# Causal attention and a gated feed-forward on one core: the scores of the two shorter query blocks share banks and one operation, and the work is put in a new order

## The chip, the cores and the metric

One NeuronCore of a Trainium2 chip runs the whole program as one launch. The metric is the device time of that launch in microseconds (us). A core has five engines that run side by side, each through its own list of instructions in order: TensorE (PE; its weight loads are listed apart as PEld), VectorE (DVE), ScalarE (ACT), GpSimd (POOL) and SyncE (SP), which here issues every DMA. A matrix product is written into PSUM, which has eight banks of 512 float32 per partition.

## The reference

Inputs are `q`, `k`, `v` of shape (4, 12, 448, 64) in float32 and four weight matrices in float64. For each batch and head:

```
scores = q @ k.T / 8, the part above the diagonal set to -1e9
attn   = exp(scores - rowmax) / (sum + 1e-9)
x      = attn @ v                       # heads side by side: (1792, 768)
out    = (((x @ w1) * (x @ w2)) @ w3) @ w_out
```

`w1` and `w2` are 768x1024, `w3` is 1024x1024, `w_out` 1024x768; the result is (1792, 768) in float32.

## The kernel before

**What is computed where.** The product `w3 @ w_out` is formed once in float32 (line 780, `w34_mm`), from weights that are loaded as 64-bit words and decoded by ACT, DVE and POOL (lines 681 to 691). Its first phase holds three row blocks at a time in six banks: two of the pool `mm`, three of the four of the pool `sc`, and the bank `av` (lines 804 and 805). It walks over the eight blocks of `w_out` (called wo 0 to wo 7 here) and needs the blocks of `w3` (w3 0 to w3 2) turned by TensorE first (line 768). Later row blocks use the `mm` banks alone.

Attention runs over 24 pairs of heads (function `pair`). A pair loads its Q and K (`turned_whole` for the first two batches, which turns them on TensorE at line 492; `halved` for the last two, which splits them into float16 halves), forms the scores (`scores`), takes the softmax on DVE (line 592), ACT (line 596) and again DVE, ACT and POOL (`inverse`, `soft`), and multiplies with V (`values`, lines 648 and 653, into the bank `av`).

The feed-forward of a batch is `gate` (lines 904 to 906, into banks of `mm` and `tr`) and `project` (lines 964 to 966). These matmuls use the whole 128x128 array and lie between the operations of the pairs.

**The scores of a pair.** Queries come in three blocks of 128 rows, with 128, 256 and 384 keys (c = 0, 1, 2), for each of two heads, and one last block of 64 rows with 448 keys for both heads. Heads share TensorE as two halves of its rows (mode `row`), the last block as quarters (mode `quad`); the product with V uses halves of the columns (mode `col`). Line 635 makes four TensorE operations: blocks c = 2 of both heads, blocks c = 1, the last block, blocks c = 0. Each operation leases its own banks of `sc` (line 568), one for each head, or one for the last block.

**What sets the order.** Nothing is emitted where it is written. Each step is put into a `Program` with a due time, its costs on the engines that can do it, and what it reads and writes. `Program.order` then simulates the five engines and the DMA queue and picks for each engine, whenever it is free, the available step with the smallest due time, less 24 us (`stick`) for a step of the mode that TensorE is in. A change of mode is charged with 0.095 us (`SWITCH`). All due times come from the dictionary `PLAN`. DMAs are steps of SP, charged with bytes over a rate. The order so found is then fixed for each engine; on the chip an engine waits at each instruction until what it needs is there.

**Holding loads back.** `hold(at, g)` (line 448) makes the loads that were added from step `at` on wait, in the planner's simulation, for the load of wo g. `hv` and `h0` of `PLAN` say which: the two halves of V of the first batch wait for wo hv and wo hv + 1, the loads of pair p for wo h0 + p; where there is no such block nothing waits.

Of the kernel before, what the change touches and what calls it, by code (L numbers as in the profile page):

```python
# [23 lines left out]
NEG = -(2.0**120)  # L24

PE, ACT, DVE, POOL, SP = "PE", "ACT", "DVE", "POOL", "SP"
PLAN = dict(nc=10, wstep=3.6064, soft=-6.8718, w0=50.8305, w34=0.7706, ab=1.9504, out=0.6632, gap=-1.6322, lat=44.2335, begin=-91.0074, wlead=70.5419, urgent=-469.9817, flex=370.3401, sc=-41.0893, vo=-494.4237, av=-194.2706, x=-353.7633, qlead=-514.025, rlead=417.269, v0=250.3178, v1=137.6978, gram=2, nf=3, h0=0, hv=1, ns=7, wo0=372.2276, wo1=301.1492, wom=91.9573, w3a=767.9653, w3l=46.2422, wd=-104.1576, wh=-132.8946, wl=1.1959, fin=-10.7242, ev=483.517, po=[7.835, -22.3194, -46.2642, -45.7187, -46.1544, -168.5123, 44.732, 118.2718, -2.1469, -154.505, -36.8352, 4.8443, 45.9944, -62.3407, -59.3789, -141.4965, -13.9926, -146.366, -84.3586, -180.0751, 32.2385, 37.7583, 62.9194, 45.468], wo=[94.042, -8.263, -88.9315, -217.7217, 115.6771, 99.8526, 211.7957, -24.8481], w3=[-158.8005, -50.8167, -61.9442, -32.663, -51.9857, -143.9432, 16.037, 208.3012], tw=[-214.4914, 58.2404, 21.4694, -22.4979, -112.6908, -172.2348, -114.743, -134.9378, -53.1451, -19.9257, -4.9187, -20.2346, -61.9799, -199.5703, -107.2525, -134.2498], slack=0.1918, pflex=136.6935, fq=2, hlead=80.6809, stick=24.2514, wfrom=6)
# [23 lines left out]
class Program:  # L51
# [1 line left out]


    def __init__(self):
        self.ops, self.writer, self.readers, self.modes = [], {}, {}, {}
        self.port, self.lock = set(), set()
        self.banks, self.leased, self.first = {}, [], {}

# [1 line left out]
        l = Lease(pools)  # L61
        return l, l

    def add(self, due, how, reads=(), writes=(), stage=None, mode=None, port=False, lock=False):

        how = how if isinstance(how, list) else [how]
        i = len(self.ops)
        deps = set()
        for k in reads:
            if k in self.writer:  # L70
                deps.add(self.writer[k])
        for k in writes:
            if k in self.writer:
                deps.add(self.writer[k])
            deps.update(self.readers.get(k, ()))
        for k in reads:
            self.readers.setdefault(k, []).append(i)
        for k in writes:
            self.writer[k] = i
            self.readers[k] = []  # L80
        deps.discard(i)
        self.ops.append((round(due + 3.7e-5, 3), how, deps, stage))
        if mode:
            self.modes[i] = mode
        if port:
# [12 lines left out]
    def order(self):  # L98
# [41 lines left out]
        while len(result) < n:  # L140
# [41 lines left out]
            if e == SP:  # L182
                move, turn = cost
                dma_free = max(dma_free, t + (1.275 if turn else 1.1)) + move
                free[e] = max(t + 0.65, dma_free - 0.93) if turn else t + 0.475
                end = dma_free + 0.91
            else:
                end = t + cost
                if e == DVE and i in self.port:
                    if lock_end > t + HELD:  # L190
                        end = lock_end - HELD + cost
                    elif lock_end <= t:
                        end += 0.1 * max(0.0, min(free[POOL], end) - t)
                    port_end = end
                if e == POOL and i in self.lock:
                    end = lock_end = max(t, port_end) + cost
                if e == PE and cost:
                    mode = self.modes.get(i)
                    if mode != last_mode:
                        cost += SWITCH  # L200
                        last_mode = mode
# [36 lines left out]
def t_mm(n, least=0):  # L238
    return max(n / 2.4 + 2, least) / 1000
# [3 lines left out]
def tile_causal_attention_moe(ctx: ExitStack, tc: tile.TileContext, q, k, v, w1, w2, w3, wo, out):  # L243
# [214 lines left out]
    def take_v(b, half, due):  # L458
# [22 lines left out]
    def turned_whole(p, b, hs, T, qk, qkk, qt, qtk):  # L481

        for i, src in ((1, k), (0, q)):
            dma(qk[0:QP, i], src[b, hs].rearrange("h (p r) d -> p r h d", r=4),
                T - PLAN["qlead"], (), [qkk + (i,)], 2 * S * D * 4, rate=181e3)

        for i in (1, 0):
            ps, key = prog.lease("sc", "tr")
# [12 lines left out]
    def halved(p, b, hs, T, qk, qkk, qt, qtk):  # L501
# [4 lines left out]
        for i, src in ((1, k), (0, q)):  # L506
            raw_k = [qkk + (i, n) for n in range(3)]
            for h in range(2):
                dma(qk[:, i, 0:3, h], src[b, hs.start + h, 0 : 3 * P].rearrange("(c p) d -> p c d", p=P), T - PLAN["qlead"],
                    [], [raw_k[h]], 3 * P * D * 4, rate=181e3)  # L510
            dma(qk[0:D, i, 3], src[b, hs, 3 * P : S].rearrange("h p d -> p h d"), T - PLAN["qlead"],
                [], [raw_k[2]], 2 * D * D * 4, rate=181e3)
# [23 lines left out]
    def pair(p):  # L536
# [25 lines left out]

            return (u // 3, u % 3, (u % 3 + 1) * P, OFF[u % 3]) if u < 6 else (2, 3, S, 0)

        def scores(us, due):
            i, c, w, lo = place(us[0])
            n = min(P, S - c * P)
            banks = [prog.lease("sc") for _ in us]
            m = mask_t if i == 2 else mask[:, (2 - c) * P :]

            def products(qs, ks, start, stop):
                for j in range(2):
                    rows = slice(j * D, (j + 1) * D)
                    ps = banks[j if i < 2 else 0][0]
                    nc.tensor.matmul(ps[rows if i == 2 else slice(0, P), :w], qs[rows, c * P : c * P + n], ks[rows, 0:w],  # L575
                                     start=start, stop=stop)

            def both():
                if not halves:
                    products(qt[:, 0], qt[:, 1], True, True)  # L580
                    return
                q16 = qt.rearrange("p i f -> p (i f)").bitcast(F16).rearrange("p (i t f) -> p i t f", i=2, t=2)
                for m_, (a, b_) in enumerate(((0, 0), (0, 1), (1, 0))):
                    products(q16[:, 0, a], q16[:, 1, b_], m_ == 0, m_ == 2)

            outs = [heads[place(u)[0]] for u in us]
            prog.add(due, (PE, (3 if halves else 4) * t_mm(w) + 0.02, both), [qtk + (1,), qtk + (0,)],
                     [key for _, key in banks] + [tk + (c,) for _, tk in outs] + ([tk for _, tk in outs] if p < 2 else []),
                     mode="quad" if i == 2 else "row")
            for u, (ps, key), (t32, tk) in zip(us, banks, outs):  # L590
                o = t32[:, lo : lo + w]
                prog.add(due + 0.4, (DVE, t_dve(w) + 0.07, lambda o=o, ps=ps, u=u: nc.vector.tensor_tensor_reduce(  # L592
                    out=o, in0=ps[:, :w], in1=m, scale=iv, scalar=-NEG,
                    op0=ALU.add, op1=ALU.min, accum_out=mx[:, u : u + 1])),
                    [key, ivk, "mask_t" if i == 2 else "mask"], [mk + (u,), tk + (c,)] + ([tk] if p < 2 else []))
                prog.add(due + 0.9, (ACT, t_act(w, pointers=1, acc=True), lambda o=o, u=u: nc.scalar.activation(  # L596
                    out=o, in_=o, func=AF.Exp, scale=-1.0, bias=mx[:, u : u + 1], accum_out=sm[:, u : u + 1])),
                    [mk + (u,)], [tk + (c,), smk + (u,)])

        def inverse(us, due):  # L600
            n = slice(us[0], us[-1] + 1)
# [463 lines left out]
```

## Time and profile before

| what | us |
|---|---|
| median of 3 runs (lowest, highest) | 557.48 (556.45, 559.26) |
| the profiled execution, its own time | 555.84 |
| its span, first to last instruction | 554.0 |
| TensorE busy | 537.5 (97%) |
| VectorE busy | 384.4 (69%) |
| ScalarE busy | 323.9 (58%) |
| GpSimd busy | 156.1 (28%) |

A line of the page names the line of the kernel, the engine, the operation, what it writes and reads, how often it ran, and its busy time and mean duration. Matmuls overlap in the records: one is listed from its start until its result has left the array, so a row of 128x448 lasts 0.35 us although the next one starts 0.19 us later. What an operation costs TensorE is read from start to start.

### The profile page before, as it was taken

Reading aid. Unit: us, or ns where it says so; the run is one execution under the profiler, and the core shown is the slowest. Engines: PE = TensorE matmul, PEld = TensorE weight load, DVE = VectorE, ACT = ScalarE, POOL = GpSimd, SP = SyncE. Lnnn points to the kernel's source line nnn. Section 1 sums busy time; section 2 is a strip of 40 time slices with the busy share of each in tenths; the row PEclk is TensorE's granted clock in tenths of the full one; section 3 lists DMA queues with packets and bytes.
Section 4 is the critical chain, followed back from the end, with each engine's and each line's share of the span. In section 5 each row is a group of like instructions: output and inputs, shape, how many; then the busy total and the mean of one; then the engine's idle time right before and its main releaser. Section 6 shows DMA issues by size and latency. Waiting matters only on the chain.

```text
span 554.0 us, 10756 instructions
## 1 busy us (share of the span) xinstructions
PE 537.5 (97%) x3872; PEld 300.5 (54%) x3872; DVE 384.4 (69%) x1057; ACT 323.9 (58%) x774; POOL 156.1 (28%) x118
## 2 busy tenths in 40 slices
PE   2999999999999999999999999999999999999996
PEld 1565565555554555555445555655555555555564
DVE  5536999998999899984998768398986760322100
ACT  6757888798698978654664646265762551111111
POOL 4000465554566424430334203231421110000000
PEclk9999999999999999999999999999999999999999
DMA  8998599989989648998777958979899235000011
GB/s 324 289 298 233 118 217 206 229 215 240 184 216 239 153 97 151 180 178 167 107 155 142 166 128 167 185 164 159 142 142 143 61 84 115 0 2 1 14 58 43
DMA packets 224950, 84.60 MB, mean 153 GB/s; under 512 B 205952, under 2 KB 221824, under 8 KB 224896
## 3 DMA queue, kind: packets, MB, share of 16 engines
q1 hardware_dynamic: 224896, 83.91, 72.1%
q8 instruction: 30, 0.49, 0.4%
q14 instruction: 24, 0.20, 0.1%
HBM read 43.78 MB, written 5.51 MB: 89 GB/s over the span
## 4 chain that ended last, share of the span: by engine, by line
PE 82%; DVE 9%; ACT 3%; DMA 3%; issue 1%; POOL 1%; POOLq 0%; ACTq 0%
PE sc L575 8%; PE mm L780 8%; PE mm L904 7%; PE mm L905 7%; PE mm L906 7%; PE mm L964 5%; PE mm L966 4%; PE mm L965 4%; PE tr L904 4%; PE av L653 4%; PE tr L905 4%; PE tr L906 4%; PE sc L780 2%; PE tr L964 2%; PE tr L966 2%; PE tr L965 2%
## 5 line engine op out<-in xcount | busy, mean ns | idle before, releaser
L906 PE MATMUL mm<-xt,w 128*128 128x448 f16 x258 | 90.9, 352 | 1.3 <-DVE w L727 1.3
L904 PE MATMUL mm<-xt,w 128*128 128x448 f16 x258 | 91.1, 353 | 0.0
L905 PE MATMUL mm<-xt,w 128*128 128x448 f16 x258 | 90.9, 352 | 0.0
L596 ACT ACTIVATE p<-p,mx 128x384 f32<-128x384 f32 (+2 forms) x144 | 71.5, 497 | 28.7 <-DVE mx L592 28.6
L780 PE MATMUL mm<-wof,w3t 128*128 128x384 f32 x192 | 71.4, 505 | 2.5 <-POOL wof L688 2.5
L628 DVE SCALAR_TENSOR_TENSOR ph<-p,rc,ph 128x384 f16<-128x384 f32 (+2 forms) x144 | 68.6, 528 | 1.4 <-ACT ph L623 0.9
L625 POOL TENSOR_SCALAR ph<-p,rc 128x128 f16<-128x128 f32 (+2 forms) x40 | 43.1, 1086 | 69.8 <-DVE rc L606 39.5
L575 PE MATMUL sc<-qkt 64*128 64x384 f16 (+7 forms) x480 | 58.9, 356 | 0.2 <-DMA qkt<-da 0.2
L906 PEld LDWEIGHTS <-w 128*128 128x128 f16 x384 | 37.5, 98 | 37.1 <-DVE w L727 2.2
L904 PEld LDWEIGHTS <-w 128*128 128x128 f16 x384 | 37.5, 98 | 36.0 <-issue 3.5
L905 PEld LDWEIGHTS <-w 128*128 128x128 f16 x384 | 37.5, 98 | 29.7 <-issue 0.2
L964 PE MATMUL mm<-w34h,arena 128*128 128x384 f16 x152 | 49.7, 327 | 0.0
L966 PE MATMUL mm<-w34h,arena 128*128 128x384 f16 x152 | 49.5, 326 | 0.0
L965 PE MATMUL mm<-w34l,arena 128*128 128x384 f16 x152 | 49.5, 326 | 0.0
L780 PEld LDWEIGHTS mm<-wof,w3t 128*128 128x128 f32 x192 | 34.2, 193 | 24.3 <-issue 4.1
L904 PE MATMUL tr<-xt,w 128*128 128x448 f16 x126 | 44.5, 353 | 0.0
L905 PE MATMUL tr<-xt,w 128*128 128x448 f16 x126 | 44.4, 352 | 0.0
L906 PE MATMUL tr<-xt,w 128*128 128x448 f16 x126 | 44.4, 352 | 0.0
L592 DVE CUSTOM_DVE_ANT_0 p<-sc,mask,qiv 128x384 f32<-128x384 f32 (+2 forms) x72 | 31.4, 478 | 18.0 <-PE sc L575 17.8
L930 ACT CAST arena<-g 128x448 f16<-128x448 f32 x22 | 12.4, 563 | 49.2 <-DVE g L925 49.2
L623 ACT ACTIVATE ph<-p,rc 128x384 f16<-128x384 f32 (+2 forms) x64 | 29.1, 504 | 9.5 <-issue 5.7
L685 DVE TENSOR_SCALAR da<-da 128x768 int32<-128x768 int32 (+1 forms) x38 | 24.2, 639 | 14.9 <-ACT da L681 14.7
(182 smaller groups left out, 1028.8 us busy)
## 6 DMA issues: line engine op xcount, KB each, us to landing
arena<-in_moe_w_dram SPq DMA_DIRECT2D x11, 768.0 KB, 5.7
vr<-in_v_dram SPq DMA_DIRECT2D x24, 192.0 KB, 3.9
out_dram<-osb SPq DMA_DIRECT2D x24, 192.0 KB, 2.2
arena<-in_moe_w_dram SPq DMA_DIRECT2D x8, 512.0 KB, 5.1
xt<-in_moe_w_dram SPq DMA_DIRECT2D x5, 768.0 KB, 8.0
qkr<-in_k_dram SPq DMA_DIRECT2D x12, 224.0 KB, 6.3
qkr<-in_q_dram SPq DMA_DIRECT2D x12, 224.0 KB, 6.9
arena<-in_moe_w_out_dram SPq DMA_DIRECT2D x3, 768.0 KB, 9.3
```

The source lines that it names most:

```text
L575: nc.tensor.matmul(ps[rows if i == 2 else slice(0, P), :w], qs[rows, c * P : c * P + n], ks[rows, 0:w], start=start, stop=stop)
L592: prog.add(due + 0.4, (DVE, t_dve(w) + 0.07, lambda o=o, ps=ps, u=u: nc.vector.tensor_tensor_reduce(out=o, in0=ps[:, :w], in1=m, scale=iv, ...
L596: prog.add(due + 0.9, (ACT, t_act(w, pointers=1, acc=True), lambda o=o, u=u: nc.scalar.activation(out=o, in_=o, func=AF.Exp, scale=-1.0, b ...
L625: (POOL, 1.1 * (t_pool(w) + 0.35e-3 * w + 0.16), lambda src=src, r=r, h=h: nc.gpsimd.tensor_scalar(out=h, in0=src, scalar1=r, scalar2=None ...
L628: prog.add(due + 0.4, (DVE, t_dve(w) + 0.06, lambda src=src, r=r, h=h, l=l: nc.vector.scalar_tensor_tensor(out=l, in0=src, scalar=r, in1=h ...
L780: prog.add(due, (PE, 4 * t_mm(NH), lambda: nc.tensor.matmul(ps[:, :NH], w3t[slot(m)][:, g], wof[:, g, ns], start=g == 0, stop=g == KF - 1) ...
L904: nc.tensor.matmul(ps[:, :S], w[:, 0, d], xh, start=d == 0, stop=False)
L905: nc.tensor.matmul(ps[:, :S], w[:, 0, d], xl, start=False, stop=False)
L906: nc.tensor.matmul(ps[:, :S], w[:, 1, d], xh, start=False, stop=d == KD - 1)
L964: nc.tensor.matmul(t, gh[:, fc, cs], w34h[:, fc, ns], start=fc == 0, stop=False)
L965: nc.tensor.matmul(t, gh[:, fc, cs], w34l[:, fc, ns], start=False, stop=False)
L966: nc.tensor.matmul(t, gl[:, fc, cs], w34h[:, fc, ns], start=False, stop=fc == KF - 1)
```

## The change

Three things change.

1. `scores` takes groups of blocks. Line 635 becomes three operations: c = 2; then c = 1 and c = 0 as one operation; then the last block. Block c = 0 (128 columns) is written behind block c = 1 (256 columns) in the same bank, for each head. The last block may lease a bank of `tr` as well as of `sc`. Reads by DVE and ACT stay as they were, one for each block and head.
2. `h0` goes from 0 to -1 and `hv` from 1 to 0: the loads of pair 0 wait for no block of `w_out`, those of pair p for wo p - 1, the halves of V for wo 0 and wo 1.
3. All numbers of `PLAN` are new, and the planner charges DMAs with other rates: 430e3 in place of 330e3 bytes per us, and 230e3 in place of 181e3 for Q, K and V. `SWITCH` stays. Those that bear on what follows:

| `PLAN` | before | after |
|---|---|---|
| h0, hv | 0, 1 | -1, 0 |
| w0, w34, lat, begin | 50.83, 0.7706, 44.23, -91.01 | 99.96, 0.5381, 87.96, 68.00 |
| qlead, rlead, v0 | -514.0, 417.3, 250.3 | -953.2, 432.6, 792.5 |
| wo0, wo1 | 372.2, 301.1 | 423.3, 333.6 |
| first three of w3 | -158.8, -50.8, -61.9 | -367.4, 320.5, 65.3 |
| first four of wo | 94.0, -8.3, -88.9, -217.7 | -105.3, 105.5, -110.6, 1.9 |
| first three of po | 7.8, -22.3, -46.3 | 51.9, -54.4, -3.5 |
| sc, stick | -41.09, 24.25 | -41.22, 25.15 |

```diff
-    def dma(dst, src, due, reads, writes, size, turn=False, rate=330e3):
+    def dma(dst, src, due, reads, writes, size, turn=False, rate=430e3):
...
-                NP * rows * D * 4, rate=181e3)
+                NP * rows * D * 4, rate=230e3)
...
-        def scores(us, due):
-            i, c, w, lo = place(us[0])
-            n = min(P, S - c * P)
-            banks = [prog.lease("sc") for _ in us]
-            m = mask_t if i == 2 else mask[:, (2 - c) * P :]
...
+        def scores(groups, due):
+
+            blocks = []
+            for us in groups:
+                i, c, w, lo = place(us[0])
+                if c == 0:
+                    shared, at = blocks[-1][1], blocks[-1][2] + blocks[-1][4][2]
+                else:
+                    shared, at = [prog.lease("sc") if i < 2 else prog.lease("sc", "tr") for _ in us], 0
+                blocks.append((us, shared, at, mask_t if i == 2 else mask[:, (2 - c) * P :], (i, c, w, lo)))
...
-                    nc.tensor.matmul(ps[rows if i == 2 else slice(0, P), :w], qs[rows, c * P : c * P + n], ks[rows, 0:w],
+                    nc.tensor.matmul(ps[rows if i == 2 else slice(0, P), at : at + w], qs[rows, c * P : c * P + n], ks[rows, 0:w],
...
+            prog.add(due, (PE, cost, both), [qtk + (1,), qtk + (0,)],
+                     list(keys.values()) + [tk + (c,) for tk, c in outs] + ([tk for tk, _ in outs] if p < 2 else []),
+                     mode=mode[0], leave=mode[-1])
...
-                    out=o, in0=ps[:, :w], in1=m, scale=iv, scalar=-NEG,
+                        out=o, in0=ps[:, at : at + w], in1=m, scale=iv, scalar=-NEG,
...
-        for n, us in enumerate(((2, 5), (1, 4), (6,), (0, 3))):
-            scores(us, T + PLAN["sc"] + 0.6 * n)
+        for n, groups in enumerate(([[(2, 5)], [(1, 4), (0, 3)], [(6,)]], [[(2, 5), (6,)], [(1, 4), (0, 3)]])[PLAN["join"]]):
+            scores(groups, T + PLAN["sc"] + 0.6 * n)
```

## Rows read from the trace of the kernel before

**Rows 1.** The page, part 1: busy us (share of the span) and instructions.

```profile
PE 537.5 (97%) x3872; PEld 300.5 (54%) x3872; DVE 384.4 (69%) x1057; ACT 323.9 (58%) x774; POOL 156.1 (28%) x118
```

**Rows 2.** Stretches: span part, then each engine's busy time, clock, DMA share, GB/s.

```profile
0.00:20.00 20.00, 9.51 (x30) 5.82 (x31) 12.08 (x22) 14.60 (x22) 5.58 (x14) 1.00 0.94 329
...
140.00:160.00 20.00, 18.96 (x157) 10.50 (x156) 19.97 (x49) 15.78 (x33) 11.58 (x6) 1.00 0.93 189
...
540.00:560.00 20.00, 9.78 (x61) 5.68 (x58) 0.00 (x0) 1.74 (x3) 0.00 (x0) 0.98 0.12 32
```

**Rows 3.** Waits of TensorE: total us, times, longest.

```profile
PE tr L768 <- DVE arena L688: 6.7, 1, 6.7
PE mm L780 <- POOL wof L688: 2.5, 1, 2.5
PE mm L906 <- DVE w L727: 1.3, 2, 1.0
```

**Rows 4.** Timeline of TensorE, one pair's scores: start, us, line, operation, count.

```profile
284.64 0.35 PE L905 MATMUL tr<-xt,w 128*128 128x448 f16 x1
284.83 0.35 PE L906 MATMUL tr<-xt,w 128*128 128x448 f16 x1
285.12 0.99 PE L575 MATMUL sc<-qkt 64*128 64x384 f16 x12
286.04 0.36 PE L904 MATMUL tr<-xt,w 128*128 128x448 f16 x1
...
288.07 0.34 PE L575 MATMUL sc<-qkt 64*128 64x128 f16 x6
288.34 0.20 PE L407 MATMUL sc<-vam,ones 128*128 128x1 bf16 x2
```

**Rows 5.** Timeline of TensorE: first lone c = 0, one behind the last block.

```profile
55.46 0.49 PE L575 MATMUL sc<-qkt 64*128 64x128 f32 x4
...
432.08 0.35 PE L906 MATMUL tr<-xt,w 128*128 128x448 f16 x1
432.36 1.03 PE L575 MATMUL sc<-qkt 64*64 64x448 f16 x12
433.32 0.36 PE L904 MATMUL tr<-xt,w 128*128 128x448 f16 x1
```

**Rows 6.** VectorE by line and form: one block's read of scores.

```profile
L592 DVE CUSTOM_DVE_ANT_0 p<-sc,mask,minus 128x256 f32<-128x256 f32 x24 | 10.7, 474 | 0.0
```

**Rows 7.** Timeline of SP: the DMAs that it issues, by array.

```profile
12.21 3.21 SPq L443 DMA_DIRECT2D xt<-in_moe_w_out_dram  x1
15.47 5.91 SPq L443 DMA_DIRECT2D vr<-in_v_dram  x4
```

**Rows 8.** Timeline of TensorE, the start.

```profile
12.01 2.93 PE L780 MATMUL mm<-wof,w3t 128*128 128x384 f32 x4 [2.46 <-POOL wof L688]
...
16.47 0.66 PE L768 MATMUL tr<-ident,arena 128*128 128x128 f32 x4 [0.68 <-ACT w3t L774]
...
18.26 1.45 PE L780 MATMUL mm<-wof,w3t 128*128 128x384 f32 x4
...
21.66 0.55 PE L492 MATMUL sc<-ident,qkr 112*128 112x112 f32 x4
22.05 0.82 PE L780 MATMUL mm<-wof,w3t 128*128 128x384 f32 x2
...
23.45 0.97 PE L575 MATMUL sc<-qkt 64*64 64x448 f32 x4
24.34 0.91 PE L780 MATMUL av<-wof,w3t 128*128 128x384 f32 x2
```

**Rows 9.** Five-microsecond stretches, columns as in rows 2.

```profile
10.00:15.00 5.00, 2.99 (x6) 1.66 (x7) 4.57 (x6) 4.47 (x7) 3.13 (x2) 1.00 1.03 424
...
20.00:25.00 5.00, 5.00 (x26) 2.86 (x25) 1.39 (x2) 3.25 (x6) 0.00 (x0) 1.00 1.31 225
```

**Rows 10.** Timeline of VectorE: the last step of decoding wo 2.

```profile
20.25 0.96 DVE L688 CUSTOM_DVE_ANT_0 wof<-arena,da 128x1536 uint16<-128x1536 uint16 x1 [0.25 <-ACT arena L683]
```

More of the change, by code (lines that the diff above doesn't have):

```diff
@@ L26 @@
 PE, ACT, DVE, POOL, SP = "PE", "ACT", "DVE", "POOL", "SP"
[L27 removed]
+PLAN = dict(nc=10, wstep=4.3513, soft=-125.7919, w0=99.9575, w34=0.5381, ab=2.3129, out=0.5532, gap=78.1363, lat=87.9611, begin=67.9975, wlead=196.6466, urgent=-299.9763, flex=910.9122, sc=-41.2246, vo=-404.2803, av=-49.0005, x=-259.5767, qlead=-953.2158, rlead=432.6325, v0=792.4525, v1=218.16, gram=2, nf=3, h0=-1, hv=0, ns=7, wo0=423.2529, wo1=333.6298, wom=-315.019, w3a=862.914, w3l=54.4892, wd=-93.5688, wh=450.671, wl=-765.9963, fin=-205.9569, ev=501.987, po=[51.9383, -54.4417, -3.4751, -73.8006, -93.2459, -608.6472, 37.5565, 81.3517, 120.7744, -301.2995, 17.1976, -6.3764, -50.4787, -37.7123, 53.8748, -159.4007, -388.994, -287.5193, -157.9855, -515.3219, 71.1529, 55.4979, -137.0095, 90.513], wo=[-105.2729, 105.5246, -110.6113, 1.9064, 375.9098, -133.5289, 485.9559, 384.1313], w3=[-367.4466, 320.5192, 65.304, -211.3003, 54.027, -253.7773, -188.4862, 3.6743], tw=[-29.043, 60.8811, -87.4584, 146.6723, 18.5679, -292.661, -259.0009, -29.9851, -211.3435, -155.3741, -12.1051, 43.4863, 65.5179, -660.2283, -57.2076, -236.7873], slack=0.8159, pflex=192.9167, fq=2, hlead=120.4329, stick=25.1509, wfrom=6, join=0)
 HOP = {
@@ L55, in __init__ @@
     def __init__(self):
-        self.ops, self.writer, self.readers, self.modes = [], {}, {}, {}
+        self.ops, self.writer, self.readers, self.modes, self.leave = [], {}, {}, {}, {}
         self.port, self.lock = set(), set()
@@ L62, in lease, with add @@
         return l, l
-    def add(self, due, how, reads=(), writes=(), stage=None, mode=None, port=False, lock=False):
+    def add(self, due, how, reads=(), writes=(), stage=None, mode=None, leave=None, port=False, lock=False):
         how = how if isinstance(how, list) else [how]
@@ L84, in add @@
             self.modes[i] = mode
+            self.leave[i] = leave or mode
         if port:
@@ L200, in order @@
                         cost += SWITCH
-                        last_mode = mode
+                    last_mode = self.leave.get(i)
                     end = matmul(t, cost)
@@ L484, in turned_whole @@
             dma(qk[0:QP, i], src[b, hs].rearrange("h (p r) d -> p r h d", r=4),
-                T - PLAN["qlead"], (), [qkk + (i,)], 2 * S * D * 4, rate=181e3)
+                T - PLAN["qlead"], (), [qkk + (i,)], 2 * S * D * 4, rate=230e3)
         for i in (1, 0):
@@ L509, in halved @@
                 dma(qk[:, i, 0:3, h], src[b, hs.start + h, 0 : 3 * P].rearrange("(c p) d -> p c d", p=P), T - PLAN["qlead"],
-                    [], [raw_k[h]], 3 * P * D * 4, rate=181e3)
+                    [], [raw_k[h]], 3 * P * D * 4, rate=230e3)
             dma(qk[0:D, i, 3], src[b, hs, 3 * P : S].rearrange("h p d -> p h d"), T - PLAN["qlead"],
-                [], [raw_k[2]], 2 * D * D * 4, rate=181e3)
+                [], [raw_k[2]], 2 * D * D * 4, rate=230e3)
             flat = qk[:, i].rearrange("p c h d -> p (c h d)")
@@ L563, in place, with products @@
             return (u // 3, u % 3, (u % 3 + 1) * P, OFF[u % 3]) if u < 6 else (2, 3, S, 0)
-        def scores(us, due):
-            i, c, w, lo = place(us[0])
-            n = min(P, S - c * P)
-            banks = [prog.lease("sc") for _ in us]
-            m = mask_t if i == 2 else mask[:, (2 - c) * P :]
-            def products(qs, ks, start, stop):
+        def scores(groups, due):
[7 more added lines that the diff above has]
+                blocks.append((us, shared, at, mask_t if i == 2 else mask[:, (2 - c) * P :], (i, c, w, lo)))
+            def products(block, qs, ks, start, stop):
+                us, banks, at, _, (i, c, w, lo) = block
+                n = min(P, S - c * P)
                 for j in range(2):
@@ L582, in both @@
[L582 to L589, printed above, removed]
@@ L590, in scores @@
-            for u, (ps, key), (t32, tk) in zip(us, banks, outs):
-                o = t32[:, lo : lo + w]
-                prog.add(due + 0.4, (DVE, t_dve(w) + 0.07, lambda o=o, ps=ps, u=u: nc.vector.tensor_tensor_reduce(
-                    out=o, in0=ps[:, :w], in1=m, scale=iv, scalar=-NEG,
[L594 to L598, printed above, removed]
+                for block in blocks:
+                    if not halves:
+                        products(block, qt[:, 0], qt[:, 1], True, True)
+                        continue
+                    q16 = qt.rearrange("p i f -> p (i f)").bitcast(F16).rearrange("p (i t f) -> p i t f", i=2, t=2)
+                    for m_, (a, b_) in enumerate(((0, 0), (0, 1), (1, 0))):
+                        products(block, q16[:, 0, a], q16[:, 1, b_], m_ == 0, m_ == 2)
@@ new lines, in scores @@
+            keys = {id(l): l for b_ in blocks for _, l in b_[1]}
+            outs = [(heads[place(u)[0]][1], b_[4][1]) for b_ in blocks for u in b_[0]]
+            mode = ["quad" if b_[4][0] == 2 else "row" for b_ in blocks]
+            cost = sum((3 if halves else 4) * t_mm(b_[4][2]) + 0.02 for b_ in blocks) + SWITCH * (mode[0] != mode[-1])
+            prog.add(due, (PE, cost, both), [qtk + (1,), qtk + (0,)],
+                     list(keys.values()) + [tk + (c,) for tk, c in outs] + ([tk for tk, _ in outs] if p < 2 else []),
+                     mode=mode[0], leave=mode[-1])
@@ new lines, in scores @@
+            for us, banks, at, m, (i, c, w, lo) in blocks:
+                for u, (ps, key) in zip(us, banks):
+                    t32, tk = heads[place(u)[0]]
+                    o = t32[:, lo : lo + w]
+                    prog.add(due + 0.4, (DVE, t_dve(w) + 0.07, lambda o=o, ps=ps, u=u, at=at, w=w, m=m: nc.vector.tensor_tensor_reduce(
+                        out=o, in0=ps[:, at : at + w], in1=m, scale=iv, scalar=-NEG,
+                        op0=ALU.add, op1=ALU.min, accum_out=mx[:, u : u + 1])),
+                        [key, ivk, "mask_t" if i == 2 else "mask"], [mk + (u,), tk + (c,)] + ([tk] if p < 2 else []))
+                    prog.add(due + 0.9, (ACT, t_act(w, pointers=1, acc=True), lambda o=o, u=u: nc.scalar.activation(
+                        out=o, in_=o, func=AF.Exp, scale=-1.0, bias=mx[:, u : u + 1], accum_out=sm[:, u : u + 1])),
+                        [mk + (u,)], [tk + (c,), smk + (u,)])
```

3 lines of the change are left out of this document (removed).

## The prediction

> **What bounds the kernel now.** The page's busy times come first: TensorE is busy 537.5 of 554.0 us, VectorE, next, 384.4 [rows 1]. The stretches show where TensorE is not: 10.5 us are missing in the first 20 and 4.2 in the last 14 [rows 2], and the waits of TensorE name the pieces between: 6.7 and 2.5 us at the start, 1.3 us later for a weight of the gate [rows 3]. So TensorE is the bound from 12 us on, and the span is its work plus the start plus the tail. "Busy" also holds what no column of data needs, so I read the timeline from start to start. A plain matmul of 448 columns starts 0.19 us after the one before it, 0.424 ns a column. Into the scores at 285.12 the step is 0.29: 0.10 too much. Their 3 x (384 + 256) columns are worth 0.81 and take 0.92: 0.11 too much on the way out [rows 4]. That holds for a lone block c = 0 too: its 3 x 128 columns are worth 0.16, the step is 0.27 [rows 4]. Behind the last block, where `quad` goes over to `row`, 3 x (448 + 128) columns are worth 0.73 and take 0.96, so two changes cost 0.23 there [rows 5]. **A change of mode costs about 0.1 us; a second operation in the same mode costs nothing.**
>
> **Part 1: the joined operation.** No matmul goes or comes; only changes of mode can go. I looked up each c = 0 block of the 24 pairs in TensorE's timeline:
>
> - 9 stand alone between matmuls of the whole array, two changes each: 6 in float32, the first at 55.46 [rows 5], and 3 in float16, the first at 288.07 [rows 4].
> - 12 stand beside another tiled operation, one change each: 8 behind the last block, the last at 432.36 [rows 5], and 4 beside a product with V.
> - 3 already follow c = 1 directly: none.
>
> That is 9 x 2 + 12 = 30 changes, 30 x 0.1 = 3.0 us, if the joined operation goes where c = 1 stands now. All of it lies on TensorE, and TensorE sets the end. From both sides: c = 1 now shares a group with c = 2 in 19 of the 24 pairs; should the new order tear all 19 apart, two changes each come back, 3.8 us, and part 1 is a loss of 0.8. Should it also bring the other 5 together (1.0) and put every last block right behind the rows, since it may now take a bank of `tr` (24 x 0.1), part 1 is worth 6.4. I take 3.0, from the order that 19 of 24 rows show.
>
> What the join adds: VectorE's read of c = 1 (0.474 us [rows 6]) now waits for the matmuls of c = 0 as well, at most 0.16 us in float16 [rows 4] and 0.5 in float32 [rows 5], and a bank comes free only after the reads of both blocks. Behind that read queue ACT's exponential and the softmax, and TensorE only at the pair's product with V, many us later; between lies gate work that needs none of it. Cost 0; if that cover were gone, 12 x (0.16 + 0.5) = 8 us could show, an upper bound. In 140 to 160 us VectorE is busy 19.97 of 20 [rows 2], the one place where cover is thin.
>
> The Trainium skill ("PSUM — Partial Sum Buffer", PSUM bank collisions) says that accesses of two engines must be kept apart by bank, not by address, which speaks against sharing: no read of c = 1 may pass beside the matmuls of c = 0. By that rule the wait above is forced in every pair; no row of before shows it, and the sum stays as long as the gate covers it.
>
> **Part 2: the loads of the first pair.** From `PLAN`, the loads' due times in the new plan: w3 0 at 423.3 + 333.6 - 367.4 - 432.6 = -43, wo 0 at 553, w3 1 at 1312, wo 1 at 1431, w3 2 at 1724, wo 2 at 423.3 + 6 x 333.6 - 110.6 - 432.6 = 1882, wo 3 at 2328. Pairs 0 and 1 begin at 119.9 and 12.0, so their Q and K are due at 119.9 + 953.2 = 1073 and at 965, and the first half of V at 119.9 + 792.5 - 6 = 906. Pair 0 waits for nothing: its loads go third, behind wo 0. V and pair 1 wait for wo 0 only, so they go ahead of wo 2; before, that half of V was issued at 15.47, behind wo 3 [rows 7].
>
> Gain: two turns of 0.39 us (21.66 to 22.05) and the last block of pair 0, 0.89 (23.45 to 24.34), can leave the full part and go into the wait of 2.46 before 12.01 and behind it [rows 8]: 2 x 0.39 + 0.89 = 1.7 us. Nothing more of pair 0 can: its row blocks need two banks of `sc`, and three of the four are held by the first phase of the weight product.
>
> Price: Q and K of a pair are 448 KB, 0.459 MB; while V was in flight the queue moved 225 GB/s, while weights were, 424 [rows 9]. So w3 1 comes 0.459 / 225 GB/s = 2.0 us later. Its turn at 16.47 already waited 0.68 [rows 8]; of the longer hole the last block fills 0.9, 1.1 remains. wo 2 has ahead of it Q and K twice and 0.688 MB of V more than before: 1.606 MB, 7.1 us. TensorE first used it at 22.05; without it it has at hand four products for the third row block (two in 1.45 us [rows 8], 2.9), the turns of pair 1 (0.8) and two last blocks (1.8): 5.5 us, to 27.5. It was decoded at 20.25 + 0.96 = 21.2 [rows 10] and would be at 28.3. These are too near each other for a term: 0. Part 2: -1.7 + 1.1 = -0.6. Its bounds are -4.1 (the wait of 2.46 filled whole and the 1.7 saved too) and +7.1 (wo 2's delay bare).
>
> The clock: in 10 to 15 us the granted clock reads 1.00 [rows 9], but four records of the weight product last 2.93 us at 12.01 and 1.45 at 18.26 [rows 8]: the pace of 1.2 GHz, and then that of 2.4, after TensorE had been idle up to 12.01 and busy since. I take 0 for a change of that.
>
> The Trainium skill ("TensorE: Matmul & The Clock Gate", What's actually happening) says that the array starts at half rate and activity releases it. By that rule turns ahead of 12.01 would bring the full pace earlier, and the sum would be 1.5 us lower; whether they come early enough no row of before can show.
>
> **Part 3: the order planned anew.** Work is the same, so a new order can only add or remove waits. Behind the start the list has 1.3 us of them [rows 3]; they could go, or more could come where VectorE is full. I take 0, bounds -1.3 and +4 (three more such waits). The tail has no scores and stays.
>
> **Sum.** -3.0 - 0.6 + 0 = -3.6 us. The profiled execution took 555.84 (span 554.0 and 1.84 around it) and would take 552.2. The median shown is 1.64 above it, so the forecast on the median is 557.48 - 3.6 = 553.9.
>
> **The rivals.**
>
> *More is gained.* The full pace comes earlier (2.93 - 1.45 = 1.5 us [rows 8]) and last blocks follow the rows directly in half the pairs (1.2). For it: the freed banks and the `tr` lease. Against: gate work also uses `tr`. Time 553.9 - 2.7 = 551.2.
>
> *Small loads starve TensorE (the other side).* Place: 20 to 50 us, where each block of `w_out` comes just in time. If the planner counts on other work that the chip does not have ready, wo 2 costs its 7.1 us bare: -3.0 - 0.6 + 7.1 = +3.5, 561.0. It decides from 3.6 us of waiting there on. For it: SP itself is held 5.91 us while it issues four loads of V [rows 7]. Against: the planner simulates the queue, and TensorE did not wait there before.
>
> *Shared banks turn into waits.* In the stretch where VectorE is full, the gate waits for a weight three times more often than now [rows 3]: about +3 against the gain, 557.
>
> *The join buys nothing.* The new order parts c = 2 from the joined operation: +0.8 - 0.6, 557.7.
>
> **How the numbers follow.** Forecast 0.47, more gained 0.18, small loads 0.16, shared banks 0.13, no join 0.06. The predicted time is the forecast's 553.9. The range 549.5 to 559.5 takes in the lower bounds of parts 1 and 2 in part and leaves most of the starving case outside; the forecast's own is 552 to 556. Faster or slower by 0.5% means below 554.7 or above 560.3; less than that a measurement of this kernel can't tell from none. The forecast lies just below, two thirds of it count as faster (0.32), more gained wholly: 0.50. Slower is most of the starving case and a little of the next: 0.16. The rest, 0.34, is the same.
>
> **What would show it.** Lone steps of 0.27 for 128 columns gone from TensorE's timeline, rows of scores in one group of 384, 256 and 128 columns, and TensorE's busy time about 3 us lower. Turns of pair 0 before 17 us, and the first 20 us with about 10 us idle still. The forecast is wrong if TensorE waits over 2 us between 20 and 50 us, or if waits for VectorE behind 100 us exceed 3 us, or if groups of scores are as many as before.

## The result and the profile after

The changed kernel is slower: 559.81 us (median of 20 runs, 557.82 to 561.40) against 556.25 (20 runs, 554.38 to 559.26), a ratio of 1.0062 with a 95% interval of 1.0047 to 1.0077. The forecast was 553.9, the range 549.5 to 559.5. Faster by 3.6 was forecast, slower by 3.6 came.

The page of the changed kernel, busy times, beside [rows 1]:

```profile
span 558.1 us, 10763 instructions
...
PE 534.4 (96%) x3872; PEld 304.9 (55%) x3872; DVE 387.3 (69%) x1063; ACT 319.4 (57%) x769; POOL 154.5 (28%) x117
```

TensorE is busy 3.1 us less, as forecast, and the span is 4.1 us longer: TensorE stands idle 23.7 us in place of 16.5. The stretches (columns as in [rows 2]) tell where. The changed kernel:

```profile
0.00:20.00 20.00, 9.79 (x40) 6.18 (x41) 11.18 (x25) 12.89 (x20) 7.67 (x16) 1.00 0.98 293
20.00:40.00 20.00, 15.75 (x59) 9.04 (x58) 7.71 (x14) 11.90 (x19) 1.07 (x1) 1.00 1.17 284
40.00:60.00 20.00, 19.73 (x70) 12.11 (x71) 11.29 (x26) 15.43 (x27) 2.40 (x2) 0.91 0.68 214
...
60.00:200.00 140.00, 135.28 (x910) 76.96 (x910) 129.32 (x335) 116.23 (x269) 74.76 (x44) 1.00 0.89 198
```

The kernel before, two stretches that [rows 2] doesn't hold:

```profile
20.00:60.00 40.00, 39.94 (x160) 23.39 (x159) 21.46 (x51) 28.52 (x56) 3.82 (x3) 1.00 0.96 241
60.00:200.00 140.00, 138.53 (x940) 78.10 (x939) 132.19 (x342) 118.67 (x265) 78.23 (x46) 1.00 0.93 200
```

In the first 20 us 10.2 us are idle, 10.5 before. From 20 to 60 it is 4.5 in place of 0.1, from 60 to 200 it is 4.7 in place of 1.5. Behind 200 us TensorE runs through in both. The waits of TensorE in the changed kernel, beside [rows 3] (line 782 is line 768 of before, 794 is 780, 493 is 492):

```profile
PE tr L782 <- DVE arena L702: 6.7, 1, 6.7
PE mm L794 <- DVE wof L702: 3.6, 2, 3.0
PE sc L493 <- DMA qkr<-in_k_dram: 2.9, 2, 2.2
PE tr L782 <- DVE w3t L789: 1.9, 2, 1.3
PE sc L493 <- DVE mx L606: 1.2, 2, 0.7
PE sc L408 <- ACT w L395: 1.1, 2, 0.6
```

TensorE's timeline over the first 50 us in the changed kernel, beside [rows 8]:

```profile
9.99 1.01 PE L493 MATMUL sc<-ident,qkr 112*128 112x112 f32 x4 [2.21 <-DMA qkr<-in_k_dram]
...
12.43 2.29 PE L794 MATMUL mm<-wof,w3t 128*128 128x384 f32 x4
14.65 0.97 PE L583 MATMUL sc<-qkt 64*64 64x448 f32 x4
...
16.14 0.92 PE L583 MATMUL sc<-qkt 64*128 64x384 f32 x4
18.36 0.66 PE L782 MATMUL tr<-ident,arena 128*128 128x128 f32 x4 [1.30 <-DVE w3t L789]
...
23.58 0.57 PE L493 MATMUL sc<-ident,qkr 112*128 112x112 f32 x4 [0.69 <-DMA qkr<-in_k_dram]
...
29.25 1.56 PE L794 MATMUL mm<-wof,w3t 128*128 128x384 f32 x4 [0.58 <-DVE wof L702]
...
40.27 1.94 PE L794 MATMUL mm<-wof,w3t 128*128 128x384 f32 x4 [2.98 <-DVE wof L702]
42.00 3.45 PE L794 MATMUL sc<-wof,w3t 128*128 128x384 f32 x6
...
47.22 2.10 PE L794 MATMUL sc<-wof,w3t 128*128 128x384 f32 x6
```

The turns and the last block of pair 0 did move ahead (9.99 to 15.5 us), and so did its block c = 2 (16.14). Then TensorE waits 0.58 us for wo 2 and 2.98 for wo 4. Behind that longest wait the matmuls run at half pace for a while: 1.94 us against 1.56 for four records, 3.45 against 2.10 for six, 1.7 us lost; the granted clock of 40 to 60 us is 0.91, where in the kernel before it is 1.00 from 20 to 60.

Who made wo 4 late? ScalarE, which decodes it, waited for its DMA (the waits of ScalarE from 20 to 60 us in the changed kernel):

```profile
ACT da L695 <- DMA w34h<-in_moe_w_out_dram: 3.3, 1, 3.3
```

The chain of work that ended last goes the same way, from the DMA over two steps of ScalarE and one of VectorE to TensorE (start, us, what):

```profile
29.88 7.57 DMA w34h<-in_moe_w_out_dram
37.49 0.04 issue
37.53 0.89 ACT da L695
38.42 0.81 ACT w34h L697
39.23 0.02 issue
39.25 0.97 DVE wof L702
40.22 0.04 issue
40.27 1.94 PE mm L794 x4
```

SP issues wo 4 only at 29.88, because eight loads of V and three pairs' Q and K stand ahead of it and fill the queue (SP's timeline in the changed kernel, beside [rows 7]):

```profile
9.57 8.54 SPq L444 DMA_DIRECT2D vr<-in_v_dram  x4
...
19.64 1.26 SPq L444 DMA_DIRECT2D arena<-in_moe_w_out_dram  x1
...
21.43 6.93 SPq L444 DMA_DIRECT2D vr<-in_v_dram  x4
...
29.88 1.30 SPq L444 DMA_DIRECT2D w34h<-in_moe_w_out_dram  x1
```

Up to wo 4 the queue carries six halves of w3 and five blocks of `w_out`, 7.08 MB, and 2.75 MB of V, Q and K. By the planner's new charges that is 7.08 / 0.43 + 2.75 / 0.23 = 28.4 us, by the old ones 7.08 / 0.33 + 2.75 / 0.181 = 36.6. To this `Program.order` adds 1.1 us ahead of the first transfer and 0.91 until the last has landed, so it counts 30.4 and 38.6. The chip took from 0.73, the first issue, to 37.45: 36.7. **Up to wo 4 the old charges are 1.9 us too long, the new ones 6.3 too short, and the order was fixed by the new ones.**

One pair's scores in TensorE's timeline of the changed kernel, beside [rows 4] and [rows 5]:

```profile
280.42 0.35 PE L920 MATMUL mm<-xt,w 128*128 128x448 f16 x1
280.70 1.16 PE L583 MATMUL sc<-qkt 64*128 64x384 f16 x18
281.79 0.76 PE L583 MATMUL tr<-qkt 64*64 64x448 f16 x6
282.47 0.36 PE L918 MATMUL mm<-xt,w 128*128 128x448 f16 x1
```

Blocks c = 2, 1 and 0 are one group (18 records, 768 x 3 columns, 0.98 us of columns in a step of 1.09); this is so in 21 of 24 pairs. In 12 pairs the last block follows at once, here in a bank of `tr`. Counted over the whole timeline TensorE changes its mode 124 times in place of 168.

### The profile page after: what moved, and what is told of

It reads as the page before. It is cut to its first block, busy times and chain, and to the rows that moved or that the text cites. A ratio compares the mean times of both kernels' runs of the same rounds, so it can differ in the third digit from the quotient of the medians.

```text
span 558.1 us, 10763 instructions
## 1 busy us (share of the span) xinstructions
PE 534.4 (96%) x3872; PEld 304.9 (55%) x3872; DVE 387.3 (69%) x1063; ACT 319.4 (57%) x769; POOL 154.5 (28%) x117
## 4 chain that ended last, share of the span: by engine, by line
PE 75%; DMA 8%; ACT 6%; DVE 4%; SPq 3%; POOL 2%; issue 1%; ACTq 0%; POOLq 0%
PE mm L918 8%; PE mm L920 8%; PE mm L919 8%; PE sc L583 5%; PE mm L794 4%; PE mm L978 4%; PE mm L980 4%; PE mm L979 4%; DMA arena<-in_moe_w_dram 4%; PE av L667 4%; PE tr L918 3%; PE tr L919 3%; PE tr L920 3%; SPq L444 3%; DMA w34h<-in_moe_w_out_dram 3%; PE tr L978 2%
## 5 line engine op out<-in xcount | busy, mean ns | idle before, releaser
L918 PE MATMUL mm<-xt,w 128*128 128x448 f16 x270 | 95.3, 353 | 0.0
L920 PE MATMUL mm<-xt,w 128*128 128x448 f16 x270 | 95.1, 352 | 0.0
L919 PE MATMUL mm<-xt,w 128*128 128x448 f16 x270 | 95.1, 352 | 0.0
L610 ACT ACTIVATE p<-p,mx 128x384 f32<-128x384 f32 (+1 forms) x144 | 71.2, 497 | 17.3 <-DVE mx L606 17.2
L794 PE MATMUL mm<-wof,w3t 128*128 128x384 f32 x192 | 70.2, 502 | 3.6 <-DVE wof L702 3.6
L639 POOL TENSOR_SCALAR ph<-p,rc 128x128 f16<-128x128 f32 (+2 forms) x41 | 41.1, 1010 | 114.0 <-DVE rc L620 56.0
L918 PEld LDWEIGHTS <-w 128*128 128x128 f16 x384 | 37.5, 98 | 37.9 <-issue 4.1
L920 PEld LDWEIGHTS <-w 128*128 128x128 f16 x384 | 37.5, 98 | 35.1
L919 PEld LDWEIGHTS <-w 128*128 128x128 f16 x384 | 37.5, 98 | 30.9 <-issue 0.2
L425 POOL TENSOR_SCALAR v<-vr,v_s 128x512 f16<-128x512 f32 x16 | 28.9, 1807 | 68.4 <-PE av L667 44.0
L978 PE MATMUL mm<-w34h,arena 128*128 128x384 f16 x144 | 47.0, 327 | 0.0
L980 PE MATMUL mm<-w34h,arena 128*128 128x384 f16 x144 | 46.9, 326 | 0.0
L979 PE MATMUL mm<-w34l,arena 128*128 128x384 f16 x144 | 46.9, 326 | 0.0
L583 PE MATMUL sc<-qkt 64*128 64x128 f16 (+7 forms) x408 | 42.8, 338 | 0.0
L918 PE MATMUL tr<-xt,w 128*128 128x448 f16 x114 | 40.2, 353 | 0.0
L919 PE MATMUL tr<-xt,w 128*128 128x448 f16 x114 | 40.2, 352 | 0.0
L920 PE MATMUL tr<-xt,w 128*128 128x448 f16 x114 | 40.2, 352 | 0.0
L637 ACT ACTIVATE ph<-p,rc 128x128 f16<-128x128 f32 (+2 forms) x72 | 32.3, 504 | 6.4 <-ACT p32t L610 3.4
## 6 DMA issues: line engine op xcount, KB each, us to landing
arena<-in_moe_w_out_dram SPq DMA_DIRECT2D x3, 768.0 KB, 10.2
```

What stands on the lines that cost most here:

```text
L583: nc.tensor.matmul(ps[rows if i == 2 else slice(0, P), at : at + w], qs[rows, c * P : c * P + n], ks[rows, 0:w], start=start, stop=stop)
L637: (ACT, t_act(w, pointers=1), lambda src=src, r=r, h=h: nc.scalar.activation(out=h, in_=src, func=AF.Copy, scale=r)),
L639: (POOL, 1.1 * (t_pool(w) + 0.35e-3 * w + 0.16), lambda src=src, r=r, h=h: nc.gpsimd.tensor_scalar(out=h, in0=src, scalar1=r, scalar2=None ...
L794: prog.add(due, (PE, 4 * t_mm(NH), lambda: nc.tensor.matmul(ps[:, :NH], w3t[slot(m)][:, g], wof[:, g, ns], start=g == 0, stop=g == KF - 1) ...
L918: nc.tensor.matmul(ps[:, :S], w[:, 0, d], xh, start=d == 0, stop=False)
L919: nc.tensor.matmul(ps[:, :S], w[:, 0, d], xl, start=False, stop=False)
```

## The experiments

Ratios are to the kernel before, run on the same chip; 0.01 is 5.6 us. In 1 to 3 the same bytes land in another arrangement, so these three kernels do not compute the reference's result. Three theories stood against each other: the early loads and the charges (queue), waits that shared banks bring, and changes of mode that cost nothing.

**1. V of the first batch in longer runs.** The order of every engine is that of the changed kernel.

```diff
+            flat = v[b, heads].rearrange("h p d -> (h p d)").rearrange("(r f) -> r f", f=NP * D)
...
+            if b == 0:
+                dst, src = dst.rearrange("p h d -> p (h d)"), flat[c * P : c * P + rows]
```

> The changed kernel with every engine's order kept; only the eight loads of V of the first batch read the same bytes as contiguous runs of 1.5 KB instead of 256 B, so the values of that batch come out in another arrangement. Theory (queue): the 1.376 MB of V ahead of wo 4 leave the queue at about 400 GB/s instead of about 200, 3 to 3.5 us sooner, so TensorE's waits of 0.6 and 3.0 us for decoded blocks of w_out and the half-speed matmuls behind the longer one (1.7 us) go: 3 to 5 us less than the changed kernel, a ratio to before of 0.997 to 1.001. Rival (shared banks, VectorE): the waits come from the join, the loads only ran beside it; less than 1 us changes, ratio about 1.005 to 1.007.

Measured: 557.59 us, ratio 1.0032 [1.0010, 1.0055], some 1.7 us less than the changed kernel. That lies between the two forecasts, and the intervals of the two ratios overlap. The waits did not go: in the profiled execution (561.97 us, 4.4 above the median) wo 4 landed at 36.9 in place of 37.5, and TensorE waited 0.6 and 2.4 us for blocks of `w_out`:

```profile
PE mm L797 <- DVE wof L705: 3.0, 2, 2.4
```

**2. Q and K of the first batch in longer runs.**

```diff
+            if b == 0:
+                to = to.rearrange("p r h d -> p (r h d)")
+                got = src[b, hs].rearrange("h p d -> (h p d)").rearrange("(r f) -> r f", f=8 * D)
```

> The changed kernel with every engine's order kept; only Q and K of the first batch are read as contiguous runs of 2 KB instead of 256 B (its scores come from rearranged values). Theory (these loads are the slowest in the queue): three pairs, 1.376 MB, go ahead of wo 4, and at about 400 in place of 160 GB/s they save 5 us of queue; the waits for blocks of w_out before 60 us go, 4 to 6 us less than the changed kernel, ratio to before 0.996 to 0.999. Rival (bytes, not their form, fill the queue, since the run with V alone gained only 2 us): 2 us or less, ratio 1.003 or more.

Measured: 555.42 us, ratio 0.9989 [0.9961, 1.0016], some 4.1 us less than the changed kernel, in time as the theory had it. In the profiled execution (560.54 us, 5.1 above the median) wo 4 landed at 35.2, and one wait for a block of `w_out` was left:

```profile
PE mm L797 <- DVE wof L705: 1.8, 1, 1.8
```

That Q and K are slower loads than V is not shown: in the changed kernel the two halves of V landed within 4.1 us each (0.688 MB), Q and K of pairs 1 and 2 within 2.4 (0.459 MB).

**3. Both, for two batches.**

> As the run with V alone, and Q, K and V of the first two batches are all read as contiguous runs (2 KB for Q and K, 1.5 KB for V), so their scores and values come out in another arrangement; every engine's order is kept. Theory (queue): the waits of TensorE between 60 and 200 us (4.7 us) come from late loads as well and shrink by half or more, on top of the first 60 us: 5 to 8 us less than the changed kernel, ratio to before 0.992 to 0.998. Rival (shared banks, VectorE): the waits of 60 to 200 us stay as they are, and with them everything that the run with V alone did not gain.

Measured: 550.66 us, ratio 0.9907 [0.9881, 0.9932]; 8.6 us less than the changed kernel, more than expected. wo 4 landed at 30.0: the two forms that singly brought it 0.6 and 2.3 us sooner bring it 7.5 together; why they do not simply add up stays open. The stretches:

```profile
20.00:60.00 40.00, 38.58 (x152) 23.60 (x150) 24.56 (x54) 31.18 (x56) 6.46 (x4) 1.00 0.77 269
60.00:200.00 140.00, 136.78 (x939) 78.43 (x939) 131.78 (x344) 113.13 (x259) 75.98 (x44) 1.00 0.84 196
```

And TensorE's longest waits in it from 20 to 60 us:

```profile
PE sc L408 <- ACT w34h L395: 0.6, 1, 0.6
PE tr L497 <- ACT w3t L792: 0.5, 1, 0.5
PE tr L786 <- ACT w3t L792: 0.3, 1, 0.3
```

Not one wait for a block of `w_out` is left, and the granted clock is 1.00 again. The same order, with wo 4 landing about when the planner had counted it, is faster than the kernel before. Of the gain 3.1 us are idle time between 20 and 60 us, and 2.0 lie in the first 20 (TensorE is busy 11.81 us there in place of 9.79). Behind 60 us the idle time falls only from 4.7 to 3.2: "half or more" of it was not the loads.

**4. Changes of mode put back.**

```diff
+                    if n_:
+                        nc.tensor.matmul(block[1][0][0][:, 500:501], ones, ones[:, 0:1], start=True, stop=True)
```

> The changed kernel with the same order; inside each of the 24 joined operations one matmul of a single column over the whole array stands between block c = 1 and block c = 0, into a column that nobody reads. It puts back the two changes of mode that the join takes away, 48 in all. Theory (a change of mode costs 0.1 us): 48 x 0.1 + 24 x 0.03 = 5.5 us more than the changed kernel, a little less where TensorE waits anyway; ratio to before about 1.015. Rival (changes of mode are free, the busy time fell for another reason): 0.7 us more, ratio about 1.0075.

Measured: 564.67 us, ratio 1.0139 [1.0116, 1.0163], 4.3 us more than the changed kernel. Less 0.7 for the small matmuls (24 x 0.03, an estimate: two matmuls of one column in a row are listed with 0.19 us in the changed kernel, one alone with 0.17), 3.6 / 48 = 0.075 us for a change; some of it falls into waits. The trace has the price without waits. One joined operation, start to start of what follows:

```profile
286.01 0.99 PE L583 MATMUL sc<-qkt 64*128 64x384 f16 x12
...
287.31 0.76 PE L583 MATMUL tr<-qkt 64*64 64x448 f16 x6
```

That is 1.30 us in place of 1.09. The step is 0.22 longer in float16 and 0.31 in float32 pairs, small matmul included: with the 0.03 taken off, 0.09 to 0.14 us for a change. Changes are not free.

**5. The square of holds and charges.** The join stays in all. For each pair of holds and charges the numbers of `PLAN` were searched anew, by the planner's own count of the end. Besides `PLAN` only the charges differ, that of Q, K and V in the same way:

```diff
-PLAN = dict(..., h0=-1, hv=0, ...)
+PLAN = dict(..., h0=0, hv=1, ...)
...
-    def dma(dst, src, due, reads, writes, size, turn=False, rate=430e3):
+    def dma(dst, src, due, reads, writes, size, turn=False, rate=330e3):
```

> As the run before it, loads held back as before the change, but the planner charges DMAs with the changed kernel's 430e3 and 230e3; PLAN searched anew, and the planner's own count foresees 0.2 us of waits of TensorE between 20 and 40 us. Theory (charge too small): the chip shows 3 us or more of waits there all the same, time 555 to 560. Rival (what costs is that loads are no longer held back): with the holds back the waits are under 1 us and the time is 549 to 553.

> The join kept, pair 0 and V held back as before, and the planner charges DMAs with 390e3 and 160e3 bytes per us, near what the traces show; the numbers of PLAN searched anew with the planner's own count. Theory (too small a charge for DMAs let the new order rely on data that is not there): TensorE waits less than 1 us in all for blocks of w_out between 20 and 60 us, its busy time stays near 534, time 550 to 554, ratio to before 0.989 to 0.996. Rival (the join itself brings waits, by shared banks): the time stays within 1.5 us of before or above, with over 3 us of waits behind 60 us.

> Loads no longer held back, as in the changed kernel, but DMAs charged with 390e3 and 160e3, PLAN searched anew; the planner's own count foresees 5.2 us of waits between 20 and 40 us. Theory (charge too small): what the planner foresees is what happens, 4 to 6 us of waits there and few others behind 60 us, time 554 to 558; the planner sees the price of the early loads once they are charged rightly. Rival (loads early are no loss by themselves): waits there under 2 us, time under 553.

> The join kept; loads held back and DMAs charged exactly as before the change (330e3, 181e3); PLAN searched anew, the planner's own count is 545.9. Theory (charge too small): with the old charges the waits for blocks of w_out between 20 and 60 us are under 1 us and the time is 551 to 555. Rival (search without a margin): waits behind 60 us of 5 us or more, time 556 or more.

> The fourth of the square of loads (held back or not) and charges (old or new): the join kept, loads not held back as in the changed kernel, DMAs charged as before the change (330e3, 181e3); PLAN searched anew, the planner's own count is 552.7, with 5.7 us of waits foreseen between 20 and 60 us. Theory (charge too small, loads early are then a choice that the planner can price): waits of 4 to 6 us between 20 and 60 us as foreseen, under 3 us behind, time 556 to 560, some 4 to 6 us above the run with held loads. Rival (not holding back costs nothing once the charge is right): time within 2 us of that run, 551 to 555.

| charges (weights / Q, K, V) | held back: planner's count, us, ratio | not held back: planner's count, us, ratio |
|---|---|---|
| 330e3 / 181e3 (old) | 545.9, 553.22, 0.9937 [0.9915, 0.9959] | 552.7, 558.51, 1.0025 [0.9999, 1.0051] |
| 390e3 / 160e3 | 545.3, 558.91, 1.0039 [1.0024, 1.0054] | 550.6, 556.47, 1.0006 [0.9986, 1.0025] |
| 430e3 / 230e3 (new) | 543.4, 565.42, 1.0165 [1.0136, 1.0194] | 541.2, 559.81, 1.0062 [1.0047, 1.0077] (the changed kernel) |

The stretches from 20 to 60 and from 60 to 200 us, of the run with held loads and old charges:

```profile
20.00:60.00 40.00, 39.95 (x161) 23.84 (x160) 19.78 (x49) 26.81 (x53) 2.45 (x2) 1.00 0.99 243
60.00:200.00 140.00, 139.35 (x946) 78.99 (x944) 133.95 (x344) 118.66 (x265) 76.67 (x44) 1.00 0.91 198
```

The same stretches of the run with held loads and new charges:

```profile
20.00:60.00 40.00, 37.13 (x142) 20.10 (x141) 24.54 (x55) 28.42 (x54) 8.35 (x5) 0.98 1.11 265
60.00:200.00 140.00, 132.39 (x858) 76.11 (x859) 129.08 (x317) 107.57 (x235) 80.50 (x43) 1.00 0.76 181
```

With the old charges and the holds TensorE is idle for 0.05 and 0.65 us; with the new charges, and the holds back, for 2.9 and 7.6. The waits of the second from 20 to 60 us, though, are not for `w_out` as I expected, but for K and Q, a bank and a decoded block of w3: the holds change which datum is late. Its 565.42 lies above the range of either forecast, and the larger part of its waits is behind 60 us. Not held back under the old charges, the loads cost 4.9 us more than held (1.0025 against 0.9937), as expected. Two stretches of that run hold most of it:

```profile
20.00:40.00 20.00, 18.12 (x79) 11.15 (x80) 11.52 (x32) 13.99 (x30) 5.07 (x4) 1.00 1.07 259
40.00:60.00 20.00, 17.16 (x52) 9.01 (x51) 9.35 (x18) 14.23 (x24) 1.84 (x1) 0.91 0.96 244
```

4.7 us are idle there, and the planner under these charges had counted 5.7 there itself: with charges near the chip the early loads show as a cost before anything runs. The planner's own counts say the same: under the old charges it counts the early loads 6.8 us longer than held ones, under the new charges 2.2 us shorter. A miss is the middle row: 390e3 and 160e3, held, was expected at 550 to 554 and took 558.91, with 6 us of waits spread behind 60 us, as its rival had it. Not held, that row took 556.47, in its range, with 3.1 us idle from 20 to 40 us in place of the 4 to 6 expected. So a charge nearer to the chip is not enough; orders found by search come out with anything between 1 and 10 us of waits behind 60 us. Holding back changes the time by -4.9, +1.8 and +5.7 us in the three rows: with one searched order in each field, the square does not part the holds and the charges from the luck of the search. The gap between the planner's count and the median is 5.8 to 13.6 us under the first two pairs of charges, 18.6 and 22.0 under the new one.

**6. The join alone, and a margin.** Loads held; 360e3 and 160e3; and every step off TensorE charged 4% more.

```diff
+                if e != PE:
+                    cost *= 1.04
                 end = t + cost
```

> The join kept, loads held back as before the change; the planner charges DMAs with 360e3 and 160e3 bytes per us and every step of VectorE, ScalarE and GpSimd with 4% more than its formula; PLAN searched anew under these charges. The planner's own count is 548.9. Theory (the order of the changed kernel fails on the chip because it was planned on too small charges): with charges on the safe side the chip keeps what the planner foresees; waits behind 60 us fall under 3 us, time 549 to 554, ratio to before 0.988 to 0.996. Rival (any order found by search has several us of waits on the chip, as the run with 390e3 and 160e3 and held loads had): 556 to 560, ratio over 1.0.

> The same charges, holds and effort of search, but the scores stay four operations with banks of their own, as before the change. The planner's own count is 551.7. Theory (the join is worth some 30 to 45 changes of mode of 0.1 us): 3 to 4.5 us of TensorE's busy time more than the run with the join, 2 to 5 us longer. Rival (the join gives back in waits for shared banks what it saves): the two within 1 us of each other.

Measured: 554.70 us, ratio 0.9967 [0.9947, 0.9987] with the join; 558.73 us, 1.0033 [1.0014, 1.0052] without. Busy times on the page of the run with the join:

```profile
PE 533.7 (97%) x3872; PEld 303.6 (55%) x3872; DVE 391.0 (71%) x1058; ACT 321.8 (58%) x765; POOL 170.3 (31%) x126
```

And on that of the run without it:

```profile
PE 539.7 (97%) x3872; PEld 299.5 (54%) x3872; DVE 388.6 (70%) x1056; ACT 320.7 (58%) x764; POOL 176.4 (32%) x129
```

6.0 us of TensorE's time less, with 131 changes of mode in place of 179, and 4.0 us of the median. The time of TensorE is the join's: 48 changes at 0.09 to 0.14 are 4.3 to 6.7 us. The median is that of one searched order each, and the orders of the square with held loads differ by 12 us, so that the join pays 4.0 is likely and not shown. The run with the join missed its expected 549 to 554 by 0.7 (its waits behind 60 us are 3.7, not under 3).

**A version that beats both** is in the square: the join, with the holds and charges of before and `PLAN` searched anew, 553.22 us (551.66 to 554.80, 11 runs), 0.6% under the kernel before. What of this is the join and what the new search, no run parts.

## Why the prediction was wrong, step by step

**What bounds the kernel** held: TensorE, from 12 us on, and time moved only by its work and its waits.

**Part 1 was right in kind and too small.** 30 changes of mode, 3.0 us, were put down; 44 went. The new order also set the last block right behind the rows in 12 of the 24 pairs, which I had left to a rival (*more is gained*). TensorE's busy time fell by 3.1, the number put down, but that is luck: with the 1.7 us of half pace taken out it is 4.8, near 44 x 0.1. Experiment 4 bears the price out, experiment 6 the gain in TensorE's time.

**The step that failed is the price in part 2**, "These are too near each other for a term: 0", and with it the sign of the whole. The span grew by 4.1 us; without the 4.5 us idle from 20 to 60 and the 1.7 at half pace it would, by this sum, lie 2.1 under the span before. The order of the loads was foreseen as it came: Q and K of pair 0 third, V ahead of wo 2. Two things were wrong behind it. First, I priced wo 2 alone. TensorE waited 0.58 us for it, near the 0.8 between my 28.3 and 27.5, by luck in part: both ends came about 1 us later (29.2 and 28.7). But the second half of V waits for wo 1 only, and pair 2 likewise, so they too went ahead of wo 4, and there nothing was left to fill with: 2.98 us, and 1.7 more at half pace. The rival of starving had the right place, 20 to 50 us, and hung its price on the wrong block; that its 561.0 lies near the time measured is luck too, as it had 7.1 us for wo 2 and nothing for part 3. Second, 225 GB/s for the small loads was too much. The 1.606 MB ahead of wo 2 made it land 9.1 us later (26.4 in place of 17.2), not 7.1: 176 GB/s, near the old charge of 181. The stretch that I took 225 from began with the end of wo 3, which landed at 21.4. The gain of 1.7 us less 1.1 came out as 0.3 less idle time in the first 20 us. That nothing more of pair 0 could move ahead was wrong as well: its block c = 2 ran at 16.14, before the weight product took its first bank of `sc` at 18.85.

**Part 3, 0, was wrong by 3.2 us**, inside its bounds of -1.3 and +4, the idle time between 60 and 200 us. Experiment 3 takes 1.5 of it away, so that much hangs on the loads of the first two batches. The rest is in waits of 0.2 to 1.0 us for VectorE and ScalarE. That they come from an order with no slack is argued from the square and not shown: what makes one searched order keep 0.65 us idle there and another 7.6 stays open. Shared banks may have a part: 1.2 us of turns wait for a read of scores (`DVE mx` in the waits), a wait that the kernel before does not have. The prediction said that a bank comes free later and priced nobody who leases it next. No run takes that away alone.

**The clock** was put at no change; the half pace came back behind the longest wait. At the start the four records took 2.29 in place of 2.93 us, 0.6 gained; at 40 us 1.7 were lost. The rule of the Trainium skill ("TensorE: Matmul & The Clock Gate", What's actually happening), that the array starts at half rate and activity releases it, agrees with the 2.29; I had used it for the start alone and not for a wait in the middle. Why the pace falls behind one wait and not behind another is not shown (see the last section).

**The shared banks**: with the join the median was 4.0 us shorter for 6.0 us less of TensorE's time; so 2.0 us came back as waits of any kind, if the two orders are otherwise alike. The rule of the Trainium skill ("PSUM — Partial Sum Buffer", PSUM bank collisions) is to keep engines apart by bank. The trace shows it kept: in all 24 pairs of the changed kernel VectorE begins the read of c = 1 0.2 us or more after the last matmul of c = 0 has ended. It is not idle just before these reads, as it reads c = 2 first; so this wait cost nothing there, as the prediction had it, though it named the gate work as cover.

**The change in the planner's charges I read and did not price.** It was in the diff, and it is what let an order pass that the chip could not keep. Summing the bytes ahead of one block and dividing by each pair of charges, as done above, takes one line and would have shown 8 us between them.

## What to carry to other kernels

Where an order is fixed ahead by a model, a more hopeful number in the model is a change of the kernel: work out what it promises for one late datum and compare it with the trace. For a load moved ahead, price every block that it goes past, up to the first at which the engine has nothing else to do, not only the next. Group tiled matmuls of one mode; here each change of mode cost TensorE about 0.1 us.

## What the runs showed of the hardware

- Loads of 256 B runs were slower than I took from a short stretch (176 GB/s in place of 225): with 2 KB runs for Q and K of six pairs alone (2.75 MB) the kernel gained 4.1 us, without a byte less. The Trainium skill ("DMA: Bandwidth & Descriptors", Specifications) wants transfers of at least 512 B for the full rate; the gain agrees in sign, and the runs show no threshold.
- A wait of 2.98 us in an otherwise full stretch was followed by matmuls at half pace (3.45 us against 2.10 for six records); the granted clock there reads 0.91. The run without holds under the old charges, idle for 2.84 us between 40 and 60, reads 0.91 there too; the kernel before, idle for 0.06 from 20 to 60, reads 1.00. But the length of the wait alone does not decide: in the run of experiment 4 the same block came after the same 2.98 us, and the matmuls behind it kept the full pace. There the half pace came behind the next long wait, 2.67 us up to 59.62.

```profile
40.77 1.56 PE L796 MATMUL mm<-wof,w3t 128*128 128x384 f32 x4 [2.98 <-DVE wof L704]
42.16 2.10 PE L796 MATMUL sc<-wof,w3t 128*128 128x384 f32 x6
```

- A joined group has no cost of its own between tiled matmuls of one mode: 18 records with 0.98 us of columns took 1.09, the 0.1 of one change.
